# A fused attention and FFT-gate kernel on one core: the last output tile in two column halves, and a new written-out order of work

## The chip, the cores and the metric

The kernel runs on one core of one Trainium2 chip. The metric is the device time of one execution in microseconds (us), with all inputs in the chip's memory at the start and the whole output written there at the end. The kernel before took 167.27 us, the median of three runs (166.73 to 167.38).

The core has five instruction queues that matter here. PE (TensorE) does the matmuls, with PEld its weight loads; DVE (VectorE) and ACT (ScalarE) do elementwise work and are the two engines that move results out of PSUM; POOL (GpSimd) makes a few small tables and issues the loads that change type; SP (SyncE) issues the remaining transfers. Each queue runs in its order, and an instruction that waits holds back everything behind it on its own queue.

## The reference

Two stages are chained. The first is attention over 4 batches, 8 heads, 768 positions and 64 channels. Each position sees the first 8 keys (global) and the 96 keys up to itself (local), with a bias that falls linearly with distance. The second takes the heads side by side as `x` (768 x 512 in each batch), projects it three ways, convolves the second projection with a filter along the sequence, multiplies by the other two, and projects out:

```python
scores = q @ k^T / 8 - slope[h] * dist ;  a = softmax(where(is_global | is_local, scores, -1e9))
x = heads_side_by_side(a @ v)                                  # 4 x 768 x 512
x1, x2, x3 = split(x @ w_proj, 3)                              # w_proj 512 x 1536
conv = irfft(rfft(x2, axis=1) * rfft(filter, axis=0), axis=1)  # circular, over 768
out = (x1 * conv * x3) @ w_out                                 # 4 x 768 x 512, float32
```

## The kernel before

**Stages.** For each batch, `attention` turns q and k so that channels lie on partitions (on PE with `turned`, L679, or for some tiles with a transposing transfer, `crossed`), makes scores (L720), takes the exponential on ACT (L748), multiplies with a mask on DVE (L760), and multiplies with v (L778, L783). In batch 0 the mask is not multiplied in. PE adds the biases of distance into the same PSUM banks ahead of the scores (L707, ten to twelve lines of `scores`), so that exp gives zero where nothing is seen. `gate` makes the first and third projections (L870, 256 matmuls of 384 columns). `conv` makes the second projection in a folded form (L944), goes to the frequency domain (L634), multiplies, comes back (L965, L968), joins halves on DVE (L1053, L1054), multiplies by the gates (L1058), and projects out (L992): six tiles `t` of 128 rows in each batch. An output tile is four matmuls of 512 columns into one bank, one move from PSUM to an `ot` buffer by ACT (L313) or DVE (L315), and one store from SP (L1000).

**The order of the work** is not left to a scheduler. `graph` records about 1030 operations; the number of an operation is its place in that record. The string `ORDER` lists them as they are to be emitted: `74P0` is operation 74 on PE with PSUM bank 0, `77A` is operation 77 on ACT, `34G` is POOL, `0S` is SP, and `i15b0` stands for 15 matmuls on zeros that only keep PE running at the start (L305). `schedule` reads the string, so the order on every engine, the choice of ACT or DVE for a move, and the banks are all written by hand or by a planner outside this file. An engine waits where an operand of its next instruction isn't there yet, or a bank or buffer is not free.

**The opening.** The first tiles of q and k come in as float32 through buffers that are later used for output: operations 0 (q0) and 2 (k0) on SP, 1 (q1) and 3 (q2) on ACT. All others come through POOL's queue, which changes them to float16 on the way: 34 is tile 1 of k ("kn1"), 41 and 42 tiles 2 and 3, 46 to 48 tiles 4 to 6; 39 and 40 are tiles 3 and 4 of q ("q3", "q4"), 45 is q5; 35 and 38 are tiles 0 and 1 of v; 52 is the first part of the gate's weights. Between these POOL makes small tables: 10 the identity, 17 and 18 a table of distances `dg`, 21 a table `far`, 7 rows of numbers. PE turns q2 in operation 74, k0 in 76, q1 in 72, q0 in 70 (all L647), kn1 in 78, q3 in 108, q4 in 110, kn2 in 112 (L679). Operations 82, 86, 90 and 94 are the biases of the four pairs of heads (L707); they need `dg`, four copies of parts of it (operations 22 to 26, L309 and L523) and a table of slopes (28 to 33). Operation 89 is the exponential of the second pair. Operations 60 to 67 are eight exponentials that make masks for batch 1 and later (L548).

In ORDER before, PE's list begins with the 15 matmuls on zeros, then 74, 76, 72, 78, 70, and the biases of 82; POOL's begins 17, 10, 34, 40, 18, 39, 7, 21, 42, 41, 35, 46, 45, 47, 48, 38, 52.

**The end.** PE's list ends with gates of batch 3, then operations 1007, 1013, 1010 (tiles 0, 2, 1), 1020, 1026 and 1023 (tiles 3, 5, 4), the moves 1027 on DVE and 1024 on ACT, and the stores.

Of the kernel before, what the change touches and what calls it, by code (L numbers as in the profile page):

```python
# [16 lines left out]
P = 128  # L17
# [18 lines left out]
def pe(*cols):  # L36
    return sum(n / 2400.0 + 0.0025 for n in cols)


ORDER = """  # L40
4V 0S 1A 2S 3A 17G 9V 28V 10G 34G 40G 11V 18G 39G 29A 7G 30A 32A 21G 19V 20V 66A 42G 41G i15b0 74P0 35G 46G 45G 13V
15V 47G 60A 48G 24A 64A 76P1 38G 52G 16V 65A 33A 25V 43G 50G 44G 49G 51G 23A 61A 72P2 8V 53G 22A 260G 259G 78P3 14V
12V 258G 77A 70P4 73V 219P1 261G 26A 82P67 79A 71A 80V 108P4 262G 63A 55G 81A 90P23 91P 31V 75A 92P 83P 109V 110P0
220A 86P45 37S 87P 111V 267G 84P 114P0 270G 93A 112P2 269G 268G 62A 85A 88P 89A 115V 67A 214P3 113V 118P67 94P45 95P
156P2 27V 215A 221V 222V 119A 96P 157V 68V 97A 122P01 154P2 120P67 123A 158P4 160P5 159A 155V 274G 121A 161V 275G 273G
276G 56G 116P01 117A 162P45 216V 217V 168P67 69V 36S 103P23 104V 105V 164P01 163A 59G 98P45 169A 165A 166P23 167A
129P67 58G 223A 99V 100V 57G 101P0 263G 130V 102V 54G 277G 106P1 124P45 131V 125V 107A 126V 170P23 266G 175P67 132P0
127P4 128A 229P5 278G 360P1 171V 491G 172V 173P2 133V 230A 135P0 139P4 140P3 228V 176V 361V 177V 231A 178P1 174A 200V
201V 232A 224A 358P5 362P2 141A 272G 142V 492G 264S 137A 134P0 179V 181P1 233V 207V 363V 364V 359A 366P45 365V 218A
136A 493G 150P2 180P0 208V 367A 143V 375P67 376A 186P3 191P4 209V 210V 203V 138V 279G 202V 204V 390P5 211V 212V 213V  # L50
205V 372P67 152A 391V 196P2 182A 188A 388P3 271G 489G 377V 389V 193A 369P45 373A 198A 436P0 437V 145P6 401P23 183A
490G 225V 226V 370A 184V 371V 506G 434P7 398P01 435V 438P4 439V 206V 374V 500G 402A 399A 400V 392P23 393A 185P7 368V
505G 449P01 450A 394V 403V 498G 451V 440P45 441A 298P2 443P01 444A 283P3 284A 187A 442V 285P4 281P5 286A 499G 147A
445V 234V 501G 395P01 282A 507G 299A 296P7 297A 289P6 290A 235V 265S 236V 307P2 308A 144P3 396A 146A 5V 237V 238V 239V
446P45 447A 190P6 149P2 151A 195P7 227A 510G 148V 192A 378P01 240V 189V 153V 197A 383P45 384V 590P2 591A 248P3 504G
249A 720G 503G 241P6 242A 448V 243P7 244A 379V 592P2 723G 385V 386P3 387A 509G 194V 457P45 397V 404P67 593A 245A 594A
380V 452P01 595A 458V 459V 405V 453V 409P23 406V 410V 381P4 454V 508G 302P5 588P6 382A 718G 411V 303A 287P4 460P5
407P7 461V 455P0 456V 589A 408A 412P1 413V 251P23 255P67 288A 250V 737G 253A 482V 257A 599P01 252A 294P4 666P7 483V
600A 295A 254V 731G 484V 300P5 719G 620P2 621V 494G 485V 301A 246P3 601V 256A 618P4 247A 305V 668P5 669A 619A 430P0
735G 664P6 733G 309P1 310A 729G 432A 665V 486V 487V 528P5 529A 721G 667A 425P4 605P23 291V 631P01 632A 292V 511P6 606A  # L60
524P5 525A 424P7 676P01 427V 512A 727G 426A 625P23 419P5 495S 304V 488V 513P6 677A 421A 311V 738G 199V 626A 514A 728G
293V 526P7 527A 312V 317P5 633V 318A 321P0 313P1 314A 306V 315P2 327P3 428V 319P4 325P6 316A 472P7 627V 326A 736G
323P5 328V 607V 324A 322V 474A 420P1 602P23 603A 320V 730G 679P45 680A 415P6 417A 422V 515P7 496S 678V 628P23 629A
330V 329V 596P45 597A 423V 331V 332V 334V 497G 734G 333V 673P01 674A 681V 725S 414P6 335V 416A 280G 473P2 630V 467P3
469A 477P4 338V 475A 463P5 622P01 516A 848S 336V 604V 623A 624V 670P23 890S 671A 889S 539P6 540A 465A 502G 478P7 847S
418V 532P0 462P1 846S 845S 533A 429P2 431A 337V 892S 819P6 820A 519P5 464A 817P0 675V 598V 520A 613P23 517P6 518A 433V
479A 468P1 726G 739G 722G 821P5 470A 480A 614V 818V 615V 537P6 340P4 608P23 538A 822A 672V 341A 339V 824A 609V 685P01
686V 687A 682P67 610V 471V 634P45 349P2 350A 683V 635V 346P3 347A 891S 684V 639P67 636V 852P01 853A 541V 640V 481V
521V 688S 348S 689S 855P45 856A 641V 616P2 352P3 353A 530P0 637P1 893P45 531A 823V 834P67 835A 617V 476V 522V 642P3
894A 466V 724S 611P2 355P0 356A 643V 857V 343P3 344A 690S 849P45 638V 612V 850A 831P67 542V 902P01 903A 660P2 659P3  # L70
523V 551P4 661A 832A 535V 654P5 662A 534V 895V 644P0 646A 552V 656A 650P4 652A 655P1 828P23 858P67 536V 657A 896P45
829A 859A 711V 351S 697P0 904V 701P1 549P2 897A 645P3 550A 543P6 712V 647A 851V 714V 702P7 713V 699A 860V 345S 555P2
898V 715V 854V 557P3 544A 658V 556A 704A 547P4 558A 649P0 833V 830V 703A 545P6 548A 757P2 836V 553P3 758A 648V 546A
357S 740P1 825P45 716V 717V 554A 560V 826A 827V 899P67 900A 744P2 651A 840P45 559V 745A 707P3 901V 709A 732G 837P67
838V 841V 561V 839A 691P0 753P2 842V 653V 696P3 754A 564V 698A 741A 562V 908P45 909V 565V 693A 905P67 864P23 755P1
563V 865V 906V 866V 910A 692P0 706P2 766P3 907V 566V 694A 861P67 862V 567V 756A 843S 844S 863V 342S 742P4 743A 759P5
760A 768P1 769A 576P0 761P5 746P1 767A 568V 569V 911S 573P3 762A 763V 764V 770V 867S 747A 579P5 748P1 912S 570P4 354S
577A 582P0 749A 765V 771V 778P1 700V 782P6 571A 774P4 583A 775A 585P7 751V 868S 705V 750V 752V 913S 580A 786P4 663V
880P0 783A 776P6 586A 777A 935V 784P5 587S 787A 779A 869P7 934V 874P6 930P1 574A 772P3 708A 695V 785A 773A 780P2 781A
937V 882A 936V 945P4 710V 938V 939A 958P3 959A 954P0 955A 789V 572S 788V 790V 940V 884P2 791A 793V 792V 794V 795V  # L80
941P3 942A 946A 943P0 944A 956P3 957A 581S 797V 967P4 796V 932A 947P0 948A 949P5 950A 968A 870P3 969P0 970A 960P1 584S
962P5 951V 952V 872A 963A 799P4 800A 879P3 961A 875P5 971V 801S 886A 871A 876A 805P4 953V 578S 877A 881A 972V 965V
992P7 993A 988P2 885P6 989A 964V 973P3 878V 974A 802P5 966V 990P2 994P3 887A 977P6 991A 883V 975P7 798V 979P1 888V
995A 873V 996V 978A 997V 575S 998V 980A 976A 981V 982V 1001V 983V 999A 1002V 814P2 815A 986V 984A 1000V 803A 6A 804S
987V 808P6 809A 929P7 919P3 806A 985V 925P2 921A 1005V 927A 924P1 926A 931A 811P5 807S 1003V 914P4 916A 1016V 812A
1006V 810S 813S 1004V 816S 920P3 928V 1018V 933V 922A 915P2 923V 917A 918V 1007P4 1019V 1017V 1008A 1013P3 1010P2
1011V 1014A 1015S 1020P3 1009S 1012S 1021A 1022S 1026P4 1027V 1028S 1023P5 1024A 1025S
"""


# [109 lines left out]
class Fused:  # L200
# [725 lines left out]
    def conv(self, b):  # L926
        nc, g, DM, S = self.nc, self.g, self.DM, self.S
        h, last = S // 2, b == self.B - 1
        g.batch = (self.PERIOD * b, self.PERIOD)
        X, y, w = self.X, self.y, self.w  # L930
        q3 = math.sqrt(0.75)
        for i in range(2):
            if (b, i) in self.PAIR_AB:
                self.projected(i)
            for t, (src, key, k) in enumerate((
# [4 lines left out]
                bk = g.bank()  # L940

                def proj(_, src=src, bk=bk):
# [7 lines left out]
                    name="ab")  # L950
# [4 lines left out]
        for jp in range(2):  # L955
            eo, ke = self.eo[:, 2 * jp:2 * jp + 2], ("eo", jp)
            for jj in range(2):
                for par, slots in ((0, (0, 1, 4)), (1, (2, 3, 5))):
                    bk = g.bank()
                    cs = slice(P * (2 * jp + jj), P * (2 * jp + jj) + P)  # L960

                    def turn(_, bk=bk, cs=cs, slots=slots, par=par):
# [11 lines left out]
                        after=self.early if b == 0 else ())  # L974
# [6 lines left out]
        for t in range(6):  # L981
            if last and t % 3 == 0:
                g.bias = 4.0 * (t // 3)
                for jp in range(2):
                    self.gated(b, (jp,), t // 3)
            if b == self.B - 2:
                g.bias = 2.0 * self.PERIOD
            bk = g.bank()

            def project(_, t=t, bk=bk):  # L990
                for c in range(4):
                    nc.tensor.matmul(bk.f32(), y[:, c, P * t:P * t + P], self.wo[:, c, :],  # L992
                                     start=(c == 0), stop=(c == 3))
            g.op("P", pe(*[512] * 4), project, acq=[bk], r=[("y", 0, t // 3), ("y", 1, t // 3), "wo"],
                 name="out")
            o = self.outs % 6
            self.outs += 1
            g.op("AV", self.evac(512), lambda e, o=o, bk=bk: self.times(e, self.ot[o], bk.f32(), osc),
                 use=[bk], w=[("ot", o)], name="ot")
            g.op("S", 0.5, lambda _, o=o, t=t, b=b: nc.sync.dma_start(  # L1000
                self.out[b, P * t:P * t + P, :], self.ot[o]), r=[("ot", o)], nbytes=(128, 2048), name="store")
            g.bias = 0.0

    def projected(self, i):
# [228 lines left out]
```

## Time and profile before

| | |
|---|---|
| median of three runs | 167.27 us (166.73 to 167.38) |
| the profiled execution | 166.88 us |
| its span, first to last instruction | 165.2 us |
| PE / DVE / ACT / POOL busy | 156.4 / 149.2 / 150.8 / 74.5 us |
| TensorE clock granted | 0.998 of full speed |
| loads and stores | 21.97 MB; the type-changing queue's packets take 98.6% of the span of 16 engines |
| stores | 24 of 256 KB, median 2.3 us from issue to landing |

The profile's times count from the first instruction of the span. "Busy" is the time in which at least one instruction of the engine was running; instructions overlap in each engine's pipeline, so a group of equal instructions is also read by the distance from one start to the next. What an engine waited for is inferred from semaphore events, and a wait is put down to the engine that came last by that reading, which can be wrong where a transfer was meant.

### The profile page before, as it was taken

What the parts mean: (1) busy time and instruction counts of PE and PEld (TensorE: products, weight loads), DVE (VectorE), ACT (ScalarE), POOL (GpSimd) and SP (SyncE); (2) the same over time, 40 slices, a digit from 0 to 9 for tenths busy, and PEclk for the clock granted to TensorE, in tenths of its full rate; (3) what the DMA queues carried; (4) which work ended last, traced back from release to release, by engine and by line L of the source; (5) the groups of instructions that cost most, each with busy time, mean ns of one, the idle gap of its engine ahead of it and who ended that gap; (6) DMA issues with size and microseconds to landing.
All of it is one profiled execution on the core that took longest, in us unless ns stands there. A gap on an engine that the chain in (4) does not pass through costs nothing.

```text
span 165.2 us, 4262 instructions
## 1 busy us (share of the span) xinstructions
PE 156.4 (95%) x1617; PEld 94.6 (57%) x1617; DVE 149.2 (90%) x334; ACT 150.8 (91%) x321; POOL 74.5 (45%) x101
## 2 busy tenths in 40 slices
PE   6499989999999999999999999999999999999990
PEld 2176678655446966465667656666754654465540
DVE  2657979999999999999999999999999998999960
ACT  4789999999999999999999999999986898999941
POOL 7999999996597999999300000000000000000000
PEclk9999999999999999999999999999999999999999
DMA  4999999999999999999995645100235160050576
GB/s 110 195 111 141 167 168 165 163 172 206 182 174 155 153 151 152 142 157 146 177 135 110 68 126 171 47 0 4 56 95 145 52 228 4 4 191 0 191 275 235
DMA packets 91540, 21.97 MB, mean 133 GB/s; under 512 B 84272, under 2 KB 88448, under 8 KB 91520
## 3 DMA queue, kind: packets, MB, share of 16 engines
q0 software_dynamic: 74960, 11.82, 98.6%
q1 hardware_dynamic: 14480, 9.37, 20.7%
q10 hardware_dynamic: 2080, 0.52, 1.7%
q8 instruction: 12, 0.20, 0.5%
q14 instruction: 8, 0.07, 0.1%
HBM read 24.64 MB, written 6.29 MB: 187 GB/s over the span
## 4 chain that ended last, share of the span: by engine, by line
PE 77%; DVE 11%; ACT 5%; issue 2%; POOL 2%; POOLq 0%; DVEq 0%; ACTq 0%
PE bank L870 22%; PE bank L992 13%; PE bank L944 8%; PE bank L720 6%; PE bank L634 6%; PE bank L679 4%; PE bank L778 4%; PE bank L783 3%; PE bank L965 3%; PE bank L825 2%; PE bank L707 2%; ACT eo L309 1%; DVE KT L309 1%; PE bank L647 1%; ACT ab L313 1%
## 5 line engine op out<-in xcount | busy, mean ns | idle before, releaser
L870 PE MATMUL bank<-xT,w 128*128 128x384 f16 x256 | 47.9, 326 | 0.0
L748 ACT ACTIVATE E<-bank 128x832 f16<-128x832 f32 (+2 forms) x64 | 44.2, 789 | 0.7 <-PE bank L720 0.5
L870 PEld LDWEIGHTS <-w 128*128 128x128 f16 x256 | 23.5, 98 | 16.2 <-issue 1.0
L325 POOL DMA_DIRECT2D vn<-in_v_dram x28 | 24.0, 867 | 2.1 <-DMA w<-in_moe_w_proj_dram 1.4
L325 POOL DMA_DIRECT2D kn<-in_k_dram x27 | 22.6, 847 | 2.1 <-PE bank L720 1.1
L992 PE MATMUL bank<-wo,y 128*128 128x512 f16 x96 | 23.0, 379 | 0.0
L760 DVE TENSOR_TENSOR E<-E,mask 128x832 f16<-128x832 f16 (+1 forms) x36 | 21.5, 622 | 0.1
L325 POOL DMA_DIRECT2D qn<-in_q_dram x21 | 19.4, 927 | 0.0
L313 ACT ACTIVATE x<-bank 128x384 f16<-128x384 f32 x32 | 17.0, 565 | 0.0
L313 ACT ACTIVATE ot<-bank 128x512 f32<-128x512 f32 x22 | 13.4, 636 | 3.3 <-PE bank L992 3.2
L313 ACT ACTIVATE ab<-bank 128x512 f16<-128x512 f32 x24 | 14.9, 665 | 1.1 <-PE bank L944 0.6
L720 PE MATMUL bank<-QT,KT 64*128 64x208 f16 (+1 forms) x224 | 15.5, 245 | 0.3 <-DVE KT L309 0.2
L802 DVE TENSOR_TENSOR xn<-bank,rc 128x512 f16<-128x512 f32 (+1 forms) x21 | 15.5, 751 | 0.2
L309 ACT CAST X<-bank 128x512 f16<-128x512 f32 x24 | 14.5, 659 | 1.0 <-PE bank L634 1.0
L879 ACT CAST g<-bank 128x384 f16<-128x384 f32 x29 | 15.3, 568 | 0.0
L992 PEld LDWEIGHTS <-y 128*128 128x128 f16 x96 | 8.9, 97 | 9.9 <-DVE y L1058 0.8
L778 PE MATMUL bank<-vn,E 128*128 128x65 f16 x224 | 14.5, 193 | 0.0
L778 PEld LDWEIGHTS <-E 128*128 128x128 f16 x224 | 13.6, 97 | 1.4
L783 PE MATMUL bank<-vn,E 128*128 128x65 f16 x192 | 14.2, 193 | 0.0
L309 ACT CAST eo<-bank 128x384 f16<-128x384 f32 x28 | 13.1, 554 | 0.6 <-PE bank L968 0.3
L783 PEld LDWEIGHTS <-E 128*128 128x128 f16 x192 | 13.0, 97 | 0.3
L720 PEld LDWEIGHTS <-KT 64*128 64x128 f16 x224 | 8.6, 94 | 7.9 <-issue 5.1
(156 smaller groups left out, 334.8 us busy)
## 6 DMA issues: line engine op xcount, KB each, us to landing
out_dram<-ot SPq DMA_DIRECT2D x24, 256.0 KB, 2.3
qn<-in_q_dram POOLq DMA_DIRECT2D x21, 128.0 KB, 5.3
vn<-in_v_dram POOLq DMA_DIRECT2D x24, 112.0 KB, 5.9
kn<-in_k_dram POOLq DMA_DIRECT2D x23, 112.0 KB, 5.6
w<-in_moe_w_proj_dram POOLq DMA_DIRECT2D x4, 256.0 KB, 5.9
ot<-in_q_dram ACTq DMA_DIRECT2D x2, 256.0 KB
w<-in_moe_w_proj_dram POOLq DMA_DIRECT2D x1, 512.0 KB, 7.2
wo<-in_moe_w_out_dram POOLq DMA_DIRECT2D x1, 512.0 KB, 7.9
```

The source lines that it names most:

```text
L309: {"A": nc.scalar.copy, "V": nc.vector.tensor_copy, "G": nc.gpsimd.tensor_copy}[e](out, in_)
L313: self.nc.scalar.mul(out, in_, c)
L325: return self.g.op(eng, 0.57 + 0.00035 * nbytes[0] if eng == "G" else 0.5, lambda _: e.dma_start(dst, src), w=w, r=r, nbytes=nbytes, name= ...
L720: nc.tensor.matmul(bs[hh].f32()[:, off:off + w], self.KT[hs, hp, P * m:P * m + P], self.QT[hs, hp, KL * m:KL * m + w], start=(off == 0 and ...
L748: nc.scalar.activation(dst, src(), Act.Exp, scale=self.scale)
L760: g.op("V", dve(w, 2), lambda _: nc.vector.tensor_mul(eo, eo, mk), r=[("mask", 2 * hp), ("mask", 2 * hp + 1)], w=[("E", hp, gi)], name="ma ...
L778: nc.tensor.matmul(o[:, n, hh], ef[:, at:at + P], vt[:, t, 2 * hp + hh, 0:D + 1], start=first, stop=(t == 0), skip_group_check=True)
L783: nc.tensor.matmul(o[:, n, hh], ef[:, at:at + P], vt[:, t - 1, 2 * hp + hh, 0:D + 1], start=False, stop=True, skip_group_check=True)
L802: nc.vector.tensor_mul(to, o[:, :, :, 0:D].rearrange("p i (t h) d -> p i t h d", h=2), rc.rearrange("p i (t h) o -> p i t h o", h=2).to_br ...
L870: nc.tensor.matmul(bk.f32()[:, 0:h], self.w[:, c, o + P * j:o + P * j + P], self.xT[:, c, h * s:h * s + h], start=(c == 0), stop=(c == 3))
L879: first = g.op("AV", {"A": act(h), "V": 0.0005}, lambda e: nc.scalar.copy(x3, pts[1].f32()[:, 0:h]) if e == "A" else None, use=[pts[1]], w ...
L992: nc.tensor.matmul(bk.f32(), y[:, c, P * t:P * t + P], self.wo[:, c, :], start=(c == 0), stop=(c == 3))
```

## The change

Two things are changed. The arithmetic stays the same.

1. In `conv`, tile `t == 5` of the last batch is made in two column halves: twice four matmuls of 256 columns, each half in a bank of its own, with its own move (two moves of 256 columns) and its own store (128 KB each). All others stay whole. This adds operations 1029, 1030 and 1031.

2. `ORDER` is replaced as a whole. 46 operations change between ACT and DVE: 25 go to DVE (4 of them, 22, 24, 26 and 33, make tables of the opening) and 21 to ACT (2 of them, 11 and 31, in the opening). One move of attention values (866, batch 3) goes from DVE to ACT, where it is eight instructions. There are 13 matmuls on zeros for 15. PE's list begins 76, 72, 70, 86, 74, 90, 78, 110, 91, 112, 88, 87, with 89 on ACT behind them; POOL's begins 21, 10, 34, 17, 41, 18, 40, 39, 42, 46, 35, 7, 47, 48, 45, 38, 52. DVE clears buffers (12, 13, 15) ahead of the tables. ACT makes all eight masks (60 to 67) ahead of its first exponential of scores; before, two of them stood between those exponentials. PE's list ends 1013, 1007, 1010, 1020, 1023, 1026, 1029; the last three moves are on ACT.

```diff
 ORDER = """
-4V 0S 1A 2S 3A 17G 9V 28V 10G 34G 40G 11V 18G 39G 29A 7G 30A 32A 21G 19V 20V 66A 42G 41G i15b0 74P0 35G 46G 45G 13V
-15V 47G 60A 48G 24A 64A 76P1 38G 52G 16V 65A 33A 25V 43G 50G 44G 49G 51G 23A 61A 72P2 8V 53G 22A 260G 259G 78P3 14V
-12V 258G 77A 70P4 73V 219P1 261G 26A 82P67 79A 71A 80V 108P4 262G 63A 55G 81A 90P23 91P 31V 75A 92P 83P 109V 110P0
...
+4V 0S 1A 2S 3A 21G 12V 13V 28V 10G 30A 29A 31A 15V 33V 11A i13b0 76P0 32A 34G 17G 19V 41G 18G 9V 40G 39G 42G 20V 66A
+63A 24V 61A 72P1 46G 14V 35G 25V 70P2 26V 23A 22V 7G 64A 47G 73A 48G 45G 67A 60A 38G 77V 86P45 80V 74P3 52G 44G 90P01
+43G 16V 75V 71A 78P2 79V 50G 49G 110P6 111V 51G 91P 81A 65A 62A 112P3 113A 88P 87P 89A 55G 261G 108P2 8V 219P6 220A
...
-1006V 810S 813S 1004V 816S 920P3 928V 1018V 933V 922A 915P2 923V 917A 918V 1007P4 1019V 1017V 1008A 1013P3 1010P2
-1011V 1014A 1015S 1020P3 1009S 1012S 1021A 1022S 1026P4 1027V 1028S 1023P5 1024A 1025S
+1013P3 1018V 916A 813S 921A 933V 918V 922A 1007P2 1008A 1016V 1009S 923V 1014A 1015S 928V 1017V 1010P7 1019V 1020P2
+1011V 1012S 1021V 1022S 1023P3 1024A 1026P7 1027A 1025S 1028S 1029P2 1030A 1031S
 """
...
-            bk = g.bank()
-
-            def project(_, t=t, bk=bk):
-                for c in range(4):
-                    nc.tensor.matmul(bk.f32(), y[:, c, P * t:P * t + P], self.wo[:, c, :],
-                                     start=(c == 0), stop=(c == 3))
-            g.op("P", pe(*[512] * 4), project, acq=[bk], r=[("y", 0, t // 3), ("y", 1, t // 3), "wo"],
-                 name="out")
             o = self.outs % 6
             self.outs += 1
...
+            past = tuple(g.readers.get(("ot", o), ()))
+            for c0, cw in ((0, DM // 2), (DM // 2, DM // 2)) if last and t == 5 else ((0, DM),):
+                bk = g.bank()
+
+                def project(_, t=t, bk=bk, cs=slice(c0, c0 + cw), cw=cw):
+                    for c in range(4):
+                        nc.tensor.matmul(bk.f32()[:, 0:cw], y[:, c, P * t:P * t + P], self.wo[:, c, cs],
+                                         start=(c == 0), stop=(c == 3))
...
+                key = ("ot", o, c0) if c0 else ("ot", o)
+                g.op("AV", self.evac(cw), lambda e, o=o, bk=bk, cs=slice(c0, c0 + cw), cw=cw: self.times(
+                    e, self.ot[o][:, cs], bk.f32()[:, 0:cw], osc), use=[bk], w=[key], name="ot", after=past)
+                g.op("S", 0.5, lambda _, o=o, t=t, b=b, cs=slice(c0, c0 + cw): nc.sync.dma_start(
+                    self.out[b, P * t:P * t + P, cs], self.ot[o][:, cs]), r=[key], nbytes=(128, 4 * cw), name="store")
```

## The prediction

> **What bounds the kernel now.** I read the page first: the busy times, the slices, and the chain that ended last. (The page's row on PE, its slices of PE, DVE and ACT, and the chain by engine.)
>
> ```profile
> PE 156.4 (95%) x1617; PEld 94.6 (57%) x1617; DVE 149.2 (90%) x334; ACT 150.8 (91%) x321; POOL 74.5 (45%) x101
> ...
> PE   6499989999999999999999999999999999999990
> ...
> DVE  2657979999999999999999999999999998999960
> ACT  4789999999999999999999999999986898999941
> ...
> PE 77%; DVE 11%; ACT 5%; issue 2%; POOL 2%; POOLq 0%; DVEq 0%; ACTq 0%
> ```
>
> Three engines are nearly full from slice 5 on, and the chain lies on PE. A busy PE may still be a slow PE, so I took distances between starts: gate matmuls (384 columns) follow each other every 163 ns, those of 512 columns every 216 ns. Distances longer than the median of their kind are waits. Past 16 us, those over 0.12 us sum to 4.8 us; the largest are 0.64 (at 22.4), 0.62 (66.9), 0.47 (73.4) and 0.37 us (32.4), all ended by DVE. So from some 24 us to the last matmul, at 161.4, PE is the bound, and hardly any of it can be saved by order. What can be saved lies at the two ends. I asked for the timeline of both.
>
> ```profile
> 0.81 0.46 SPq L325 DMA_DIRECT2D ot<-in_q_dram  x1
> 0.81 1.25 ACTq L325 DMA_DIRECT2D ot<-in_q_dram  x2
> ...
> 1.26 4.73 PE L305 MATMUL bank<-idle 128*128 128x512 f16 x15 [1.26 <-DVE idle L369]
> ...
> 1.33 0.57 SPq L325 DMA_DIRECT2D ot<-in_k_dram  x1
> ...
> 8.15 1.46 PE L647 MATMUL bank<-p,ot 128*128 128x128 f32 x12 [2.16 <-DVE vn L1124]
> ...
> 12.39 0.86 ACT L748 ACTIVATE E<-bank 128x832 f16<-128x832 f32 x1
> ```
>
> PE idles 2.16 us before its first useful matmul. The trace names a memset on DVE as the releaser; it is not one. The first matmuls of PE's list turn q2, and the last landing event of that load comes at 8.02 us, 0.13 before the start. The last landing events of the others: q0 at 4.95, q1 at 5.87, k0 at 7.07. The windows show how full the engines are after that (columns: window and its length, then busy time of PE, PEld, DVE, ACT, POOL).
>
> ```profile
> 8.00:12.00 4.00, 3.85 (x44) 2.98 (x45) 2.43 (x11) 3.50 (x10) 4.00 (x6) 1.00 1.74 111
> 12.00:16.00 4.00, 4.00 (x58) 2.34 (x53) 2.74 (x7) 4.00 (x9) 4.00 (x6) 1.00 2.16 142
> 16.00:20.00 4.00, 4.00 (x65) 2.60 (x66) 3.64 (x9) 4.00 (x7) 4.00 (x5) 1.00 1.57 166
> 20.00:24.00 4.00, 3.52 (x82) 2.77 (x78) 3.09 (x8) 3.75 (x9) 4.00 (x5) 1.00 2.16 166
> ```
>
> From 12.4 to 24 us ACT is full with twelve exponentials and PE waits for it in many small pieces; DVE has room.
>
> **The opening, step by step.** PE now turns k0 first: 7.07 + 0.13 = 7.20 us, which is 0.95 earlier. 13 matmuls on zeros end by about 5.6 (the two left out took 0.216 each), so they are no obstacle, and the gap before useful work shrinks from 2.2 to 1.6 us.
>
> The price is on POOL. `far` (1.24 us from its first row to its last, at 6.27 to 7.51 before) goes ahead of everything from 0.91: the identity ends at 2.8 (before 1.56), kn1 is issued at 2.8 (1.60), kn2 at 3.95, `dg` is done at 6.05 (4.69), q4 is issued at 6.0 (2.58), q3 at 6.9 (4.63). From there the queue has the same issues up to 14.0 as before, so later loads are not moved. Do the late ones hurt?
> - kn1: in the trace POOL's first packets start near 6.5, once those of SP and ACT thin out (ACT's last go by at 7.0), though kn1 was issued at 1.60. A later load, kn3, shows the unhindered way: issued 7.45, first packets near 9.4, landed 10.86. With 2.0 us to its first packet, an issue at 2.8 is still early enough; kn1 lands at 8.4 as before (8.47), kn2 near 8.9.
> - q4: packets from 8.0 (6.0 + 2.0; the 1792 packets ahead, at some 1220 in each us, end then too), 1024 packets are 0.84, and the last landing follows 0.85 later (q3: 0.83): 9.7. Its bounds are 9.4 (kn3's 3.41 from issue) and 12.4 (its own 6.36 of before). Behind its turn, 110, PE's list holds all that ACT's first exponential needs (91, 112, 88, 87).
> - `dg`: DVE's two edits and the first mask follow it by 0.94 in the trace, so masks start at 6.99 and DVE's copies at 6.95.
>
> Then by engine. PE: k0 to 7.6, q1 to 8.05, q0 to 8.5 (four matmuls of 0.109 each). DVE: five pieces for the biases (22, 24, 26 at some 0.3 each, 0.30 and 0.24 for the memset and L523) to 8.4. So PE does biases 86 from 8.5 to 8.95 (0.46 in the trace), q2 to 9.4, biases 90 to 9.86, kn1 to 10.05, q4 to 10.3 (landed 9.7), and a score, kn2 and the scores of 89 until some 10.8. DVE's moves of k0, q2 and kn1 are done near 10.5. ACT has ahead of its first exponential, from 6.99 on: eight masks (0.283 each, 2.26), one copy (0.39), the moves of q1 and q0 (0.51 each), the global keys (0.25) and kn2 (0.43), together 4.35; so that exponential starts at 11.35, against 12.39: 1.04 earlier. Behind it, ACT has 10.8 us until the last exponential, where before it had 11.3 (two masks and a k move are gone from there, one L413 has come). So ACT leaves the opening 1.04 to 1.56 earlier, PE enters it 0.95 earlier. PE and DVE set what follows, so I take 1.1, near PE's row. Bounds: +0.5 us (a loss) if q4 lands at 12.4 and holds PE's list, 1.6 us gained at best.
>
> **The end.** (The last rows of the timeline, and the page's row of stores.)
>
> ```profile
> 156.01 5.38 PE L992 MATMUL bank<-wo,y 128*128 128x512 f16 x24
> ...
> 161.47 0.60 ACT L313 ACTIVATE ot<-bank 128x512 f32<-128x512 f32 x1 [1.18 <-PE bank L992]
> ```
>
> ```profile
> out_dram<-ot SPq DMA_DIRECT2D x24, 256.0 KB, 2.3
> ```
>
> Now: last matmul ends 161.39; move 161.47 to 162.07; store issued 162.09; landed 164.12 (2.02 later: 0.33 issue, 0.53 to the first packet, 0.80 of packets, 0.35 to the last event); then 1.0 us of closing semaphores. After, with T the end of tile 4's matmuls: halves end at T+0.43 and T+0.87 (216 against 2 x 108 ns, four more weight loads beside matmuls). ACT moves tile 4 at T+0.09; its next may start 0.48 later (distance of 512-column moves), at T+0.57; the last, of 256 columns, runs T+0.95 to T+1.34 (0.60 less 128-column steps of 0.11 each, estimated 0.39). Before, T+1.55. But SP has three issues in a row, of 0.33, 0.42 and 0.42 (rows of stores behind each other) with 0.05 between: T+0.71, T+1.09, T+1.54, where the only one of before stood at T+1.57. So the earlier move gains nothing, and the gain is in the packets: half of 0.80 less, but behind the other two stores' 1.2 us of packets (0.80 and 0.40 from T+1.57), which end at T+2.8. Last landing T+2.8+0.4+0.35 = T+3.5, against T+3.6; if the first packets come without queuing, T+3.2. Gain 0.1 to 0.3; I take 0.2. The third store of a row took 2.5 to 2.7 us in the trace, so a loss of 0.1 is the other bound.
>
> On the half store a page of the Trainium skill speaks against the change: "DMA: Bandwidth & Descriptors", section "Anatomy of one DMA", gives a transfer (fitted on POOL's path) a fixed cost of about 2.0 us whatever its size, and only bytes / 436 GB/s on top, by which 128 KB less save 0.3 us. The trace's store has only 1.2 us outside its packets. By the page the end would come out 0.1 us worse than by the row; no run here shows a half store yet.
>
> **The middle.** Priced by the distances of equal rows, the moves between ACT and DVE past the tables give DVE some 0.8 us more (k moves 0.9, an x move 0.47, tables 0.7, less 0.6 for xn 866, 0.6 for q moves) and ACT 0.5 (866 alone: eight at 0.196). DVE is busy 149.2, so this is half a percent of it. What the new order does to PE's 4.8 us of waits the trace can't say. The lists give one sign: PE operations that stand directly behind the DVE or ACT operation they need were 20, and are 15. I take no change; the bounds are half the waits gone (-2.4) and six new ones (below).
>
> **Sum.** 1.1 + 0.2 = 1.3. Against the profiled execution: 166.88 - 1.3 = 165.6 us. That execution lies 0.4 under the median of 167.27, so the median to expect is **166.0 us**.
>
> **Rivals.**
> - *The opening's gain is eaten* (22%): PE starts early, but the scores wait for inputs that come when they came. For it: POOL is full from 8 to 32 us, and w's first part is issued at 14.0 as before. Against it: ACT, not landings, ends the waits from 12 to 24. Only the end is left: 167.1.
> - *PE ahead of DVE, slower* (13%): at 66.9 PE's L944 waits 0.62 for L853, at 73.4 L965 waits 0.47 for L1095. If the new order meets these two in each of the three later batches, that is six waits of 0.55, 3.3 us: 169.3. It decides for slower from four such waits on (2.2 against the 1.3 gained and the 0.8 of the bound). For it: DVE is busy 8.00 of 8 us in two windows past 80, and gets 0.8 more. Against it: the later batches show none now, and the list has fewer close pairs.
> - *The middle improves too* (10%): the waits halve, 163.6.
> - *The change doesn't do what it says*: if q2's landing were not what PE waits for, PE would start at 8.15 still. I count that in the first rival.
>
> **How the numbers follow.** Forecast 55%, rivals 22, 13 and 10. Half a percent, 0.84 us, is what a measurement of this kernel can tell. Of the forecast, four fifths are beyond it (opening over 0.65): faster 0.44 + 0.10 = 0.54; same 0.11 + 0.20 = 0.31; slower 0.13 + 0.02 = 0.15. The range: at the low end 1.6 + 0.3 and a fifth of the waits, 1.0, from 167.3: 164.4; at the high end the opening's loss of 0.5 and the end's of 0.1, 167.9. It leaves out the slower rival and half of the third, 18%.
>
> **What would show it.** PE's first L647 at 7.2 and bound to k0; the first L748 near 11.35 and the last of batch 0 over a us earlier; `dg` at 6.05 and q4 landed by 9.7; the last store's landing 3.5 after tile 4's matmuls; PE's waits past 16 us again near 5. I am wrong if q4 lands past 11, if PE's waits past 24 us grow by two us, or if the store of 128 KB also takes 2.0.

## The result, and the profile after

The changed kernel takes 165.18 us (median of 8 runs, 164.94 to 166.21), the kernel before 167.38 beside it (8 runs, 166.73 to 167.93). The ratio is 0.9883, 95% interval 0.9854 to 0.9911: 2.0 us faster by the ratio, where 1.3 was forecast. The profiled execution took 165.6 us with a span of 163.9, against 166.88 and 165.2, so the two traces show 1.3 us of it; that of before lies 0.5 under its median here, that of after 0.4 over its own.

The page of the changed kernel (PE's and DVE's rows, the chain by engine, the row of stores):

```profile
PE 156.0 (95%) x1619; PEld 95.3 (58%) x1619; DVE 149.6 (91%) x339; ACT 149.7 (91%) x325; POOL 73.9 (45%) x101
...
PE   6798999999999999899999999999999999999990
...
PE 55%; DVE 25%; POOL 6%; ACT 5%; DMA 4%; issue 2%; POOLq 0%; ACTq 0%; DVEq 0%
...
out_dram<-ot SPq DMA_DIRECT2D x23, 256.0 KB, 2.5
```

The busy times have hardly moved. The chain now goes over DVE for a quarter of the span, yet PE's waits of over 0.12 us past 24 us sum to 3.97 us, against 3.91: which engine the chain passes over does not say how long anybody waited. The opening, from the timeline:

```profile
7.16 1.45 PE L647 MATMUL bank<-p,ot 112*128 112x112 f32 x12 [1.14 <-DMA ot<-in_k_dram]
...
8.54 0.35 PE L707 MATMUL bank<-dg,eo 64*128 64x416 bf16 x1
...
11.61 0.87 ACT L748 ACTIVATE E<-bank 128x832 f16<-128x832 f32 x1
...
12.05 0.91 POOL L325 DMA_DIRECT2D qn<-in_q_dram  x1
```

PE starts at 7.16 (7.20 forecast, 8.15 before), the biases stand at 8.54 (8.5), the first exponential at 11.61 (11.35; 12.39 before). The last row is q5's load. Its packets land as late as 17.97; in before it was issued at 10.73 and landed at 15.23.

```profile
PE bank L647 <- DMA ot<-in_k_dram: 1.1, 1, 1.1
PE bank L679 <- DVE KT L309: 0.6, 1, 0.6
PE bank L679 <- DMA qn<-in_q_dram: 0.2, 1, 0.2
```

These are PE's waits from 7 to 24 us (in total, times, longest): for k0; at 15.8 us for a key move that stands behind the spread of the masks on DVE; and at 18.0 for q5.

To see where time is won, I asked at each moment how much of PE's work was left: every matmul not yet started, counted with the median distance of its kind. What the changed kernel has less to do than before is PE's **lead**, in us (the columns e2 to e11 are experiments below; all against the same trace of before):

| at us | after | e2 order only | e8 q2 first | e9 scores apart | e11 spread later |
|---|---|---|---|---|---|
| 8 | 0.81 | 0.82 | 0.00 | 0.71 | 0.71 |
| 16 | 0.01 | 0.02 | -0.54 | 0.02 | 0.47 |
| 24 | 0.31 | 0.37 | -0.91 | -0.46 | -1.00 |
| 32 | 0.20 | 0.20 | -1.26 | -0.61 | -1.43 |
| 56 | 1.56 | 1.60 | 0.06 | 0.06 | 0.27 |
| 104 | 1.01 | 1.51 | 0.43 | -1.04 | -0.06 |
| 152 | 1.35 | 1.79 | 0.49 | -0.81 | 0.06 |

The opening's lead of 0.8 us is there at 8 us and gone at 16. From 32 to 56 us the lead grows by 1.36 us, in a stretch for which nothing was forecast.

### The profile page after: what moved, and what is told of

Its sections match the earlier page's. It is cut to its first block, busy times and chain, and to the rows that moved or that the text cites. A ratio compares the mean times of both kernels' runs of the same rounds, so it can differ in the third digit from the quotient of the medians.

```text
span 163.9 us, 4281 instructions
## 1 busy us (share of the span) xinstructions
PE 156.0 (95%) x1619; PEld 95.3 (58%) x1619; DVE 149.6 (91%) x339; ACT 149.7 (91%) x325; POOL 73.9 (45%) x101
## 4 chain that ended last, share of the span: by engine, by line
PE 55%; DVE 25%; POOL 6%; ACT 5%; DMA 4%; issue 2%; POOLq 0%; ACTq 0%; DVEq 0%
PE bank L870 16%; PE bank L996 12%; PE bank L944 8%; DVE E L760 5%; PE bank L634 4%; DMA qn<-in_q_dram 4%; DVE xn L802 3%; PE bank L720 3%; PE bank L778 3%; PE bank L965 3%; POOL kn L325 3%; PE bank L783 2%; PE bank L707 2%; ACT E L748 1%; DVE xT L309 1%
## 5 line engine op out<-in xcount | busy, mean ns | idle before, releaser
L870 PE MATMUL bank<-xT,w 128*128 128x384 f16 x256 | 48.5, 326 | 0.6 <-DVE KT L309 0.6
L748 ACT ACTIVATE E<-bank 128x832 f16<-128x832 f32 (+2 forms) x64 | 44.6, 785 | 1.2 <-PE bank L720 1.2
L870 PEld LDWEIGHTS <-w 128*128 128x128 f16 x256 | 23.6, 98 | 17.1 <-issue 1.9
L325 POOL DMA_DIRECT2D vn<-in_v_dram x28 | 23.4, 852 | 4.0 <-DMA wo<-in_moe_w_out_dram 1.7
L996 PE MATMUL bank<-wo,y 128*128 128x512 f16 (+1 forms) x100 | 22.9, 370 | 0.0
L879 ACT CAST g<-bank 128x384 f16<-128x384 f32 x30 | 15.8, 542 | 0.3 <-PE bank L870 0.3
L313 ACT ACTIVATE x<-bank 128x384 f16<-128x384 f32 x31 | 16.1, 548 | 0.0
L313 ACT ACTIVATE ot<-bank 128x512 f32<-128x512 f32 (+1 forms) x23 | 12.9, 608 | 3.1 <-PE bank L996 1.9
L802 DVE TENSOR_TENSOR xn<-bank,rc 128x512 f16<-128x512 f32 (+1 forms) x20 | 15.2, 763 | 0.2
L778 PE MATMUL bank<-vn,E 128*128 128x65 f16 x224 | 15.3, 193 | 0.0
L778 PEld LDWEIGHTS <-E 128*128 128x128 f16 x224 | 14.0, 97 | 1.9
L783 PE MATMUL bank<-vn,E 128*128 128x65 f16 x192 | 15.0, 193 | 0.0
L720 PE MATMUL bank<-QT,KT 64*128 64x208 f16 (+1 forms) x224 | 14.9, 245 | 0.0
L783 PEld LDWEIGHTS <-E 128*128 128x128 f16 x192 | 13.2, 97 | 0.8 <-issue 0.2
L309 ACT CAST eo<-bank 128x384 f16<-128x384 f32 x28 | 12.4, 566 | 0.8 <-PE bank L968 0.8
L720 PEld LDWEIGHTS <-KT 64*128 64x128 f16 x224 | 8.4, 94 | 6.4 <-issue 3.9
```

What stands on the lines that cost most here:

```text
L309: {"A": nc.scalar.copy, "V": nc.vector.tensor_copy, "G": nc.gpsimd.tensor_copy}[e](out, in_)
L313: self.nc.scalar.mul(out, in_, c)
L325: return self.g.op(eng, 0.57 + 0.00035 * nbytes[0] if eng == "G" else 0.5, lambda _: e.dma_start(dst, src), w=w, r=r, nbytes=nbytes, name= ...
L720: nc.tensor.matmul(bs[hh].f32()[:, off:off + w], self.KT[hs, hp, P * m:P * m + P], self.QT[hs, hp, KL * m:KL * m + w], start=(off == 0 and ...
L748: nc.scalar.activation(dst, src(), Act.Exp, scale=self.scale)
L778: nc.tensor.matmul(o[:, n, hh], ef[:, at:at + P], vt[:, t, 2 * hp + hh, 0:D + 1], start=first, stop=(t == 0), skip_group_check=True)
```

## The experiments

Three theories at first. A, the prediction: the opening gives 1.1 us, the halves 0.2. B: the opening's lead is lost by 16 us and the later order makes the gain. C: the opening's lead sits in ACT and DVE and comes out later. All ratios are to the kernel before, run beside them. e2 was not run again beside e5 to e12; where these are set against it, it is by the ratios.

**e1 and e2: the two parts of the change alone.** e1 has the order of before with the last tile in halves, e2 the new order with the last tile whole.

```diff
e1:
-1026P4 1027V 1028S 1023P5 1024A 1025S
+1023P5 1024A 1026P4 1027A 1025S 1028S 1029P3 1030A 1031S
e2:
-1023P3 1024A 1026P7 1027A 1025S 1028S 1029P2 1030A 1031S
+1023P3 1024A 1026P7 1027A 1025S 1028S
```

> The order of before throughout; only the last tile is made in two halves (its operations at the very end, behind tile 4, moves on ACT). Theory A (the prediction: the opening gives 1.1 us, the end 0.2): 0.2 us faster than before, last landing 3.4 after tile 4's matmuls end. Theory B (read from the changed kernel's trace, where the last landing comes 2.73 us after the last matmul in both kernels: the end gives nothing, three stores in a row use up what the halves save): within 0.1 us of before, ratio 1.000.

> The new order without the halves: the last tile is one piece again. A: 0.2 us slower than the changed kernel, so 2.0 us faster than before (ratio 0.988). B: as fast as the changed kernel or a little faster, 2.2 us under before (ratio 0.987).

e1: ratio 0.9994 (0.9973 to 1.0015). e2: 0.9881 (0.9854 to 0.9908). The whole gain is in the order; the halves give nothing that can be measured.

**e3 and e4: the new order's opening alone, and its rest alone.** The list is cut behind batch 0's last exponential.

```diff
e3: the new ORDER up to 169A, then what is left in the order of before
e4: the ORDER of before up to batch 0's last exponential, then what is left in the new order
```

> The new order up to the last exponential of batch 0, then the order of before for all that is left; last tile whole. A (opening): 1.1 us faster than before. C (the opening's lead sits in ACT and DVE at first and reaches PE later, whatever the later order): 1.2 to 2 us faster, PE hardly ahead at 24 us and over 1 us ahead at 56. B (PE in the changed kernel is only 0.3 us ahead at 24 us, the gain is made by the later order): 0 to 0.4 us faster.

> The order of before up to the last exponential of batch 0, then the new order for all that is left; last tile whole. A and C: within 0.4 us of before. B: 1.2 to 2 us faster than before, the lead growing between 32 and 56 us.

e3: 1.0108 (1.0072 to 1.0143). e4: 1.0083 (1.0058 to 1.0108). Both are slower, which no theory had: the orders load the quarters of w in different turns (operations 53 and 55), so after the seam the first gates wait for a quarter that comes second. The trace of e3 shows 1.51 us on it (PE's longest wait on L870, for the load of w, at 30.7 us). These two say nothing on the question.

**e5 and e6: the same with operations 53 and 55 exchanged in the first part.**

```diff
e5 (as e3):
-55G 261G ... 53G
+53G 261G ... 55G
e6 (as e4):
-53G ... 55G
+55G ... 53G
```

> The new order through batch 0's last exponential, then the order of before, as in the run with the new opening alone, but the second quarter of w that is loaded early (at 19.0 us) is the one that the order of before needs first, so that the wait of 1.5 us on w at 30.7 us should be gone. Theory A (the opening's 1.1 us is carried to the end): ratio 0.993. Theory C (the opening's lead sits in ACT and DVE and comes out later): also 0.993, but with PE's lead at 0 at 16 us and above 0.6 from 40 us on. Theory B (the lead is lost by 16 us and the gain is made by the later order): 0.999 to 1.001, PE's lead within 0.4 us of zero from 16 us to the end.

> The order of before through batch 0's last exponential, then the new order, with the early quarter of w (at 19.5 us) being the one that the new order needs first. Theory B: ratio 0.988 to 0.992, PE's lead growing between 32 and 56 us and again near 75 us to 1.3 us or more. Theories A and C: 0.998 to 1.001. If the stall on w at 30.6 us stays at over 1 us, then the wait is not on the order of the quarters and the split is again undecided.

e5: 1.0038 (1.0017 to 1.0060). e6: 0.9986 (0.9966 to 1.0006). The wait for w is gone, but neither half carries the gain, so they are no sum: together 0.9881. In e6 PE waits 1.2 us at 24.4 us on L778, directly behind the seam, for the last exponential: the new rest wants early what the old opening delivers last.

```profile
PE bank L778 <- ACT E L748: 1.2, 1, 1.2
```

What can be used is the lead away from the seam: from 32 to 56 us it grows by 1.65 us in e6 and by 0.04 in e5. The gain of that stretch belongs to the new rest. (The trace of e5 is of its fastest execution, 166.45 us against a median of 167.94, so it shows where PE's work lies and not the loss.)

**e7 and e11: the opening's two stalls taken away.** e7 moves the masks' spread (69) behind the key moves and q5's load (45) ahead of kn5 and kn6 (47, 48); e11 moves the spread alone. Both are on e2.

```diff
e7, e11: 69V is taken from in front of 221V 157V and put behind 155V
e7 alone:
-47G ... 48G 45G
+45G 47G ... 48G
```

> The new order with the last tile whole, and two operations of the opening moved: the spread of the masks of heads 4 to 7 (1.6 us on DVE) behind the key moves that PE waited for at 15.8 us, and q5's load ahead of kn5 and kn6 on POOL's queue, as before, so that it lands some 1.7 us sooner. If these two stalls (0.77 and 0.34 us) are what eats the opening's lead of 0.8 us (theory B's account of the opening): PE's lead at 24 us is 0.8 to 1.2 and the ratio 0.981 to 0.985, against 0.988 without the moves. If ACT, full with exponentials, is what holds PE there (theory C): the waits come back in front of other matmuls, PE's lead at 24 us stays below 0.5 and the ratio at 0.987 to 0.989.

> The new order with the last tile whole, with only the spread of the masks of heads 4 to 7 (1.6 us on DVE at 13.4 to 15.0) moved behind the key moves that PE waits for at 15.8 us; q5's load stays where the new order has it. Theory B's account (DVE's list eats the opening's lead): the wait of 0.77 us at 15.8 is gone and PE's lead at 16 us is 0.5 or more; 0.3 to 0.7 us faster than the new order, ratio 0.984 to 0.986. If the landings of the key loads and q5 are what holds PE there (theory F): PE waits for a landing instead, at 15.6 and at 18.0, and the ratio stays at 0.987 to 0.990.

e7: 0.9978 (0.9950 to 1.0006). e11: 0.9938 (0.9917 to 0.9958). Both lose against e2. PE's waits from 7 to 24 us in e7 and then in e11:

```profile
PE bank L679 <- DMA kn<-in_k_dram: 1.2, 2, 0.9
PE bank L707 <- DVE xn L802: 1.0, 1, 1.0
PE bank L647 <- DMA ot<-in_k_dram: 0.3, 1, 0.3
```

```profile
PE bank L707 <- DVE xn L802: 1.2, 1, 1.2
PE bank L647 <- DMA ot<-in_k_dram: 0.9, 1, 0.9
PE bank L679 <- DMA qn<-in_q_dram: 0.9, 1, 0.9
```

The wait on DVE at 15.8 goes in e11, and at 18.2 PE waits 0.9 for q5; with q5 ahead, the keys behind it are late (0.9 at 17.6). Whichever load is last of these three holds PE until about 18 us: theory F is right, and DVE's list alone did not eat the lead. The rest of the loss is the edit's own: the two spreads now run one behind the other on DVE, from 19.0 to 21.9 us, and the first division (L802), which PE needs at 22.9, starts at 22.15 instead of 20.55. Whether the spread has a place that costs nothing was not tried.

**e8: the opening's start undone.** e2 with q2's turn first on PE's list again.

```diff
-76P0 32A ... 74P3
+74P3 76P0 32A ...
```

> The new order with the last tile whole, where PE's list begins with q2's turn again, so that the first useful matmul starts at 7.96 us (q2's landing of 7.83 and 0.13) instead of 7.16. Theory A (the earlier start is carried through): 0.8 us slower than the new order, ratio 0.993. Theory B (that lead is lost by 16 us whatever is done): no difference, 0.987 to 0.989.

0.9951 (0.9924 to 0.9978): 0.7% or 1.2 us slower than e2 (the intervals don't overlap).

```profile
8.19 1.89 PE L647 MATMUL bank<-p,ot 128*128 128x128 f32 x16 [1.30 <-DMA ot<-in_q_dram]
...
13.10 0.87 ACT L748 ACTIVATE E<-bank 128x832 f16<-128x832 f32 x1
```

PE starts at 8.19, and the first exponential at 13.10, 1.5 us after e2's (11.60). So B is wrong on the opening, and A right on its mechanism: the early start is carried to the end. What I had called a lost lead is the early start paying for what the rest of the new opening costs; without it PE is 0.5 us behind the kernel before at 16 us. C falls as well: what grows later grows with the old opening too (e6).

**What grows between 32 and 56 us?** The waits don't: from 32 to 56 us before has a single one in the view of waits, of 0.2 us. So I added up, pair by pair of neighbouring lines, what each distance has over the median of its kind. From 32 to 56 us those parts between 60 and 300 ns sum to 2.74 us in before and to 1.60 in e2. Most stand where scores (L720) meet another kind: 2.56 of the 2.74 us in before lie at 21 such places, 0.12 each. PE's timeline in before, then in e2, over the same kind of work:

```profile
40.39 0.35 PE L720 MATMUL bank<-QT,KT 64*128 64x208 f16 x4
40.67 0.82 PE L870 MATMUL bank<-xT,w 128*128 128x384 f16 x4
41.43 0.62 PE L720 MATMUL bank<-QT,KT 64*128 64x208 f16 x12
41.98 1.04 PE L944 MATMUL bank<-w,xcf 128*128 128x512 f16 x4
43.00 0.40 PE L720 MATMUL bank<-QT,KT 64*128 64x208 f16 x6
```

```profile
41.01 1.04 PE L944 MATMUL bank<-w,xcf 128*128 128x512 f16 x4
41.88 1.03 PE L944 MATMUL bank<-w,xo 128*128 128x512 f16 x4
42.75 1.03 PE L944 MATMUL bank<-w,xr 128*128 128x512 f16 x4
43.71 0.84 PE L720 MATMUL bank<-QT,KT 64*128 64x208 f16 x18
44.48 1.04 PE L944 MATMUL bank<-w,xr 128*128 128x512 f16 x4
```

Read the starts, not the lengths. In before, four gate matmuls at 163 ns are 0.65 us, and 0.76 pass until the scores start (40.67 to 41.43). Twelve score matmuls run as six pairs side by side, two heads on 64 rows each: four pairs at 89 ns and two narrow ones at 42 are 0.44, and 0.55 pass. Four L944 matmuls at 216 are 0.86, and 1.02 pass. Each change between 64 and 128 rows costs 0.11 to 0.16 us, and no engine stands as its cause. In e2 the first two L944 groups follow each other with 0.87 us each, which is no loss, and 0.96 pass from the third to the scores.

The weight loads (PEld) show where the price comes from. Past 30 us in before, where one kind of 128-row matmul follows another (L870, L944, L634), the first load of the new kind starts 0.16 to 0.22 us ahead of its matmul, beside the matmul before it. At 40 or more of the 44 changes to or from scores it starts only 4 to 5 ns ahead, and a load takes 0.09 to 0.10 us: by these rows the price has the size of a weight load that nothing hides. "TensorEngine Tiling (Array Packing)" of the Trainium skill, section "Key Properties", states the rule without a price: a change of tiling mode drains TensorE. The trace agrees that a change costs time, 0.11 to 0.16 us here; no run tells a drain from the load that is not hidden.

In batch 1 the list of before has eleven separate runs of scores, the new one seven: eight changes fewer, 8 x 0.12 = 1.0 us. Over the whole list it is only four fewer, 60 for 64, because the new opening has four more up to 16 us; from 56 us on both traces have 22. That these changes make the gain of the stretch is theory D; theory E puts the gain into DVE's and ACT's order.

**e9: take runs of scores apart again.** e2, with nine pairs of neighbours in batches 1 and 2 separated by one other PE operation (four of the nine):

```diff
-369P67 ... 375P45 ... 390P3 135P2
+369P67 ... 390P3 135P2 375P45
-366P23 373A 392P45 191P1
+366P23 373A 191P1 392P45
-605P45 294P3
+294P3 605P45
-679P45 ... 676P67 419P2
+679P45 ... 419P2 676P67
...
```

> The new order with the last tile whole, but in batches 1 and 2 nine runs of score matmuls are taken apart again: one other PE operation (a gate, a projection, an inverse turn) is put between two scores that stood together, so that the list has 78 changes between scores (L720, 64 rows) and other matmuls instead of 60. Theory D (each such change costs PE 0.10 to 0.15 us, because the weights of the next matmul are not loaded beside the last one, and the new order's gain past 24 us is that it has fewer of them): 18 x 0.12 = 2.2 us slower than the new order, ratio 1.000 to 1.003, with the excess on rows L720 next to others up by about 2 us. Theory E (the gain past 24 us lies in the order of DVE and ACT, and the changes between kinds of matmul are hidden): no difference, 0.986 to 0.990.

0.9994 (0.9977 to 1.0012): 1.9 us slower than e2, 0.10 us for each of the 18 changes, where 2.2 was expected. The parts of 60 to 300 ns past 16 us grow from 6.85 to 9.06 us. In this profiled execution q5 lands at 18.8 us, which takes 0.8 us before the edit begins; from 32 us to 152 the lead falls by 0.20 where e2's rises by 1.59, and the difference of 1.8 is the edit's. The same 56 score matmuls between 32 and 56 us show the number of runs, since the drawn-out end of each run counts as busy (the sum line of L720 over three windows of 8 us: before, after, e9):

```profile
sum 24.00, PE 4.23 PEld 1.88; mean PE 1.41 PEld 0.63
```

```profile
sum 24.00, PE 3.53 PEld 1.91; mean PE 1.18 PEld 0.64
```

```profile
sum 24.00, PE 4.22 PEld 1.74; mean PE 1.41 PEld 0.58
```

The new order has shortened these rows by 0.7 us, and e9 brings them back to what they were. Nor is it later exponentials that make e9 slow: distances of more than 0.3 us over their median sum to 1.0 us past 24 us in e9, and to 1.1 in e2. Theory D stands, but it is not all of the stretch from 32 to 56 us: in e9, whose trace has 22 changes there against 21 in before, the lead still grows by 0.67 us, against 1.40 in e2.

**e10 and e12: more grouping.** e10 groups three scores of batch 1 in the list of before, e12 two places in e2.

```diff
e10: 366P45 behind 180P0; 372P67 behind 388P3; 401P23 behind 434P7
e12: 372P67 in front of 366P23; 438P7 in front of 395P23
```

> The order of before with three score operations of batch 1 moved by one or two PE operations, so that they stand next to other scores: 58 changes between scores and other matmuls instead of 64. Theory D: 6 x 0.12 = 0.7 us faster than before, ratio 0.994 to 0.997. Theory E: 0.999 to 1.002. If the later exponentials of the moved scores hold PE, the ratio is over 1.002 and new waits of over 0.3 us stand between 30 and 50 us.

> The new order with the last tile whole, and two moves on PE's list in batch 1: the score 372 stands behind the gate 180, next to 366 and 392, and the k turn 438 stands ahead of the score 395, so that 395 and 398 are neighbours. The list has 56 changes between scores and other matmuls instead of 60. Theory D: 4 x 0.12 = 0.5 us faster than the new order, ratio 0.984 to 0.986, a version ahead of both kernels. If the later exponentials hold PE, as in the order of before with three scores moved: new waits of over 0.3 us on L748 between 30 and 50 us and a ratio of 0.988 to 0.992.

e10: 1.0041 (1.0025 to 1.0057). e12: 0.9914 (0.9883 to 0.9944), no better than e2 (the intervals overlap). PE's waits from 32 to 48 us in e10, then e12; before and e2 have no wait on L748 there:

```profile
PE bank L720 <- ACT E L748: 0.4, 1, 0.4
PE bank L870 <- ACT E L748: 0.3, 1, 0.3
```

```profile
PE bank L720 <- ACT E L748: 0.3, 1, 0.3
PE bank L679 <- ACT x L313: 0.2, 1, 0.2
```

In e12 the parts of 60 to 300 ns from 32 to 56 us fall from 1.60 to 1.13 us, which is the 4 x 0.12 that was expected, and 0.87 us of new waits come in (two distances, 0.39 us over the median at 37.7 us and 0.48 at 39.2). A score that starts later hands ACT its exponential later. So the price of a change is not the only term: scores can be grouped as far as ACT doesn't run out of work. None of the runs beats the new order; e2 is level with the changed kernel.

## Why the prediction was right, and where it was wrong

The time lay in the range and the sign was right. Even the sum for the profiled execution, 165.6 us, was met exactly, but by errors that cancel; that is luck. By PE's lead, the 1.27 us between the spans divide like this:

| term | forecast | measured |
|---|---|---|
| opening (lead at 32 us) | 1.1 | 0.20 |
| 32 to 56 us | 0 | 1.36 |
| 56 us to the last matmul | 0 | -0.34 |
| end | 0.2 | 0.05 |

- **PE's start: right; POOL's prices: right to half a us.** 7.16 for 7.20; POOL's list ran a little ahead of the reckoning (kn1 issued at 2.50 for 2.8, q4 at 5.53 for 6.0), and the landings were as forecast: kn1 landed at 8.29 (8.4), kn2 at 8.82 (8.9), q4 at 9.65 (9.7), the masks began at 6.51 (6.99). That k0's landing and not the memset ended PE's idle time shows in e8: with q2 first it is 8.19 again. The rival in which the change doesn't do what it says is out.
- **"From there the queue has the same issues up to 14.0 as before, so later loads are not moved": this step failed.** The set is the same, its order is not. q5 went from 10.73 to 12.05, behind kn5 and kn6, and landed at 17.97 instead of 15.23. Of these 2.74 us, 1.32 are the later issue; the rest is that its parts landed far apart, the first 1.16 us later than before (15.33 for 14.17), the last 2.74. In the order of before a load issued at 12.4 (kn6) landed anywhere from 16.57 (e6) to 19.36 us (e1), so q5's new place is one where landings differ from one execution to the next. I had looked at the names in the queue and at its end, not at each place in it. e7 shows that it can't simply be undone: the three loads are wanted at one time, and the last of them is late.
- **"I take 1.1, near PE's row": too much by 0.9 at 32 us.** The first exponential came 0.78 earlier instead of 1.04, and PE's 0.8 was spent by 16 us on DVE's list and at 18 on q5. ACT did not leave the opening 1.04 to 1.56 earlier either: it was through with its masks at 10.58 and waited 0.60 for kn2's turn on PE, and at 16.9 it waited 1.06 for scores that stand behind PE's stall at 15.8:

```profile
16.88 5.24 ACT L748 ACTIVATE E<-bank 128x832 f16<-128x832 f32 x8 [1.06 <-PE bank L720]
```

ACT's last exponential of batch 0 starts at 23.64, against 23.71 before, where over a us was forecast. This is near the first rival, which I had at 22% and which gave 167.1; but q5 comes later than before, not when it came, and e8 shows that without the early start the opening would have been a loss.
- **"Hardly any of it can be saved by order" and "I take no change" for the middle: the main error.** I had counted distances over their median from 0.12 us on, 4.8 us in all, and taken the rest for PE's own pace. After the change those waits are 4.5. But the parts from 60 to 120 ns sum to 5.2 us past 16 us in before, and nobody releases them, so no view of waits shows them. 3.4 of the 5.2 stand at changes between 64 and 128 rows on PE, and those depend on the order. The lists that I had (where I counted close pairs of PE and DVE) would have given it: eleven runs of scores against seven. The third rival, at 10%, had the right place and a wrong mechanism, waits halved.
- **The end: the size was wrong.** From the end of the matmuls of the last tile but one (T) to the end of the span, before has 4.64 us, e2 (whole tile) 4.60, after 4.59. The last rows of ACT's moves:

```profile
159.38 1.21 ACT L313 ACTIVATE ot<-bank 128x512 f32<-128x512 f32 x3 [1.53 <-PE bank L996]
```

T is 159.30. The last of these three moves ends at T+1.29 (1.34 forecast), but SP's three issues in a row end later than reckoned: the last starts at T+1.63 (1.54), its first packet goes at about T+2.8 behind the other two stores' packets, and it lands at T+3.60, as the single store of before and the last half store of e1. From issue to landing the half store took 1.97 us, the whole one 2.02. That was on my list of what would make me wrong. My row's sum, T+3.5, was off by 0.1; the 0.2 that I took was the middle of a range whose better end had the packets come without queuing. The estimate by the Trainium skill ("DMA: Bandwidth & Descriptors", section "Anatomy of one DMA"), in which half a store saves only 0.3 us, came nearer, at T+3.6; no run here shows a half store that does not queue, so whether its split holds stays open.
- **PE ahead of DVE, slower: out.** PE's waits past 24 us are 3.97, against 3.91; at 66.1 and 75.0 us one each stands, as before, and no more.

What stays open: the two halves of the order don't add up (e5, e6), and only part of this is shown, the seam's wait for the last exponential. Of the 1.36 us from 32 to 56, 1.14 are in the parts of 60 to 300 ns; the count of changes there (21 before, 14 after in the trace) explains 7 x 0.12 = 0.84 of them; what makes the 0.67 us by which the lead of e9 grows there is not shown. The 0.7 us between 1.3 in the traces and 2.0 in the times is where the two profiled executions lie in their spread. q5's landing differed by 2 us between traces with the new order of loads (16.96 in e8, 19.0 in e3), which is enough for such a spread, but no run ties the two together.

## What to carry to other kernels

On a full engine, add up all distances over the median of their kind, the small ones too, and by pair of neighbouring lines: what no semaphore ends appears in no view of waits. Where a kernel mixes matmuls on 64 and on 128 rows, count the changes between them in the order and keep runs together, as far as the engine that they feed does not run dry. And when an order is rewritten, compare a queue place by place: the same loads in another turn are other loads.

## What the runs showed of the hardware

- A change between score matmuls on 64 rows and matmuls on 128 rows costs PE 0.10 (e9, from the times) to 0.16 us (the timeline of before), while PE counts as busy. The first weight load behind it starts 4 to 5 ns ahead of its matmul, where between kinds on 128 rows it starts 160 to 216 ns ahead (before, past 30 us).
- A 128 KB store, third in a row on its queue, took 1.97 us from issue to landing, where a 256 KB store, 0.8 us behind the one before it, took 2.02: its own packets are half as long (47 ns for 87), and it waited for the others'.
- In e2, POOL's loads issued before 11 us land their 16 parts within 0.8 to 0.9 us of each other, and those whose first part lands between 15 and 20 us within 1.9 to 2.6 (q5 in after: 15.33 to 17.97); in before it is 0.8 to 1.9 us for the latter. A wait for the whole load is a wait for its slowest part.
